# A group's choice of experts in two parts around a tile's decay, and the ranking of the experts behind the second expert's first block

## The chip, the cores and the metric

The kernel runs on one core of one Trainium2 chip. Its time is the device time of one launch in microseconds (us), the median of the runs of one kernel. Engines are named as in the profile: PE is TensorE (PEld its weight loads), DVE is VectorE, ACT is ScalarE, POOL is GpSimd, SP is SyncE, which here only issues transfers.

## The reference

Retention with a decay per head, and a two-level mixture of experts that takes one expert for each token:

```python
scores = scale * q @ k.T                          # batch 8, heads 8, seq 576, head_dim 64
ret = scores * where(rel >= 0, gamma[h] ** rel, 0)
x = (ret @ v), heads side by side                 # 4608 tokens x 512
g_logits = x @ w_group                            # 4 groups
g_idx, g_w = argmax and its softmax share
e_logits = x @ w_expert[g_idx]                    # 4 experts in a group
e_idx, e_w = argmax and its softmax share
h = relu(x @ w1[g_idx, e_idx])                    # 512 -> 1024
out = g_w * e_w * (h @ w2[g_idx, e_idx])          # 1024 -> 512
```

## The kernel before, in words

All engines run in a written order: the helper `Ordered` (L112) pins each instruction of VectorE, ScalarE, POOL and SP behind the one issued before it in the program, and TensorE's order is the program's too. So an engine that waits holds up all that is queued behind it.

**The tile loop** (L871, `t` from 0 to 36) goes over 36 tiles of 128 tokens. In iteration `t`, TensorE sums tile t-1's products of scores and values into `px` (`av`, L816), sums the running state of tile t (`state`, L801), adds the earlier tokens' part to `px` (`inter`, L834) and computes the scores of tile t+1 (`scores`, L760 and L772). VectorE multiplies `px` with the decay into `xT` (`turned`, the one instruction that is called the decay below; the next tile's `av` writes the same PSUM) and masks the scores of tile t+1 out of PSUM into `sT` (`masked`; the scores of tile t+2 write the same PSUM). ScalarE scales the values (`vs`), copies the state (`st`) and copies turned rows with their weight (`xt`). Tile t-6 is turned back (`xnat`, L369) and its rows are stored to a list per expert in HBM (`xs`) by POOL.

Three tiles are a group. Two iterations after its last tile come its logits (`logits`, L411), one later their turning (`gate_pe`, L424), one later, in iterations 6, 9, ..., 33, and 35 for the group before the last, the choice (`choose`, L427): seven steps on VectorE, `lg`, `mx`, `df`, then `oh`, `m2`, `oh`, `ob`, and an exponential of `df` on ScalarE between them. In the same iteration the weights of the rows follow (`weigh`, five steps that end in `wt`), and TensorE's sums for the places of the rows in their lists (`places_pe`, L498 to L502), which read `ob`; the next iteration computes the places (`places`, three steps). VectorE's order in such an iteration is: choice, decay, weights, masks. TensorE's is: `av`, `state`, `inter`, scores, `xnat`, logits where due, place sums.

**The transition** (L1106 to L1164) does the last group's logits and choice and the last six tiles' stores, picks the second expert (`pick(1)`; the first one was picked earlier, and its pass 0 runs here in blocks of 128 hidden columns), pads and reads expert 1's rows. `rank_experts` (L954) is a generator in three parts on VectorE: the order of all experts, their sizes and masks, and the addresses of the padding. Its first part runs in pass 0 behind `ids(0)`, the second ahead of expert 1's block 0, the third behind block 1. `expert_of(2)` lets SP read expert 2's number from that order.

**The passes** (L1168): an expert has 8 blocks (`p`, `f`); each is `layer1` (L602, 12 products into `ph`), ScalarE's relu `hh` and VectorE's remainder `hl`, and, one block later, `layer2` (L1028 to L1030). The weights come in pieces of two blocks and are split by ScalarE (`wh`) and VectorE (`wl`) three half pieces ahead. Expert 2's padding (`xpad(2)`, POOL) is issued in block 2 of expert 1, the read of its rows (`xload(2)`, SP) in block 3, their turning (`xturn`, VectorE, which writes `xTf`) in block 5 and their split (`xsplit`, `xTh` and `xTl`) in block 6.

Of the kernel before, what the change touches and what calls it, by code (L numbers as in the profile page):

```python
# [16 lines left out]
RG = 3  # L17
# [21 lines left out]
NT = N // P  # L39
# [30 lines left out]
def moe_retention(ctx, tc, qk, kv, wgt, w1, w2, c_f, out):  # L70
# [286 lines left out]
    def xnat(t, pool_=None):  # L357
        xnat_pe(t, pool_)
        xnat_out(t)
        xnat_store(t)  # L360
# [60 lines left out]
    def gate_pe(t):  # L421
        pl = ps_sm.tile([P, RG, P], F32, name=f"pl_{t}", tag="sm")
        for x_ in range(RG):
            pe.transpose(pl[:, x_, :], tiles[t]["lt"][:, x_, :], ident)  # L424
        tiles[t]["pl"] = pl

    def choose(t):  # L427

        pl = tiles[t]["pl"]

        def t_(nm, shape, dt=F32):
            return sm.tile([P, RG] + shape, dt, name=f"{nm}_{t}", tag=nm)

        K = G + 1
        n = RG
        lg = t_("lg", [GE])
        dve.tensor_reduce(
            lg, pl.rearrange("p r (a g) -> p r g a", a=NKC)[:, :, 0:GE], AX.X, ALU.add
        )
        lv = lg.rearrange("p r (k e) -> p r k e", e=4)  # L440
        mx = t_("mx", [K])
        dve.tensor_reduce(mx, lv, AX.X, ALU.max)
        df = t_("df", [K, 4])
        dve.tensor_tensor(df, lv, mx.unsqueeze(3).to_broadcast([P, n, K, 4]), ALU.subtract)
        ex = t_("ex", [K, 4])
        act.activation(ex, df, AF.Exp)
        oh = t_("oh", [K, 4])
        dve.scalar_tensor_tensor(
            oh.rearrange("p r k e -> p (r k) e"), df.rearrange("p r k e -> p (r k) e"), 0.0,
            rank.unsqueeze(1).to_broadcast([P, n * K, 4]), ALU.is_ge, ALU.mult,  # L450
        )
        m2 = t_("m2", [K])
        dve.tensor_reduce(m2, oh, AX.X, ALU.max)
        dve.tensor_tensor(
            oh, oh, m2.unsqueeze(3).to_broadcast([P, n, K, 4]), ALU.is_equal
        )
        tiles[t]["rt"] = ex, oh
        ob = obs[-1][:, 1:, :]
        dve.tensor_tensor(
            ob.rearrange("p r (g e) -> p r g e", g=G), oh[:, :, 1:, :],  # L460
            oh[:, :, 0, :].unsqueeze(3).to_broadcast([P, n, G, EG]), ALU.mult,
        )
# [42 lines left out]
    def places(t):  # L505
        n = RG
        ob = obs[-1]
        of = ob[:, 1:, :]
        pp = tiles[t]["pp"]
        pr = sm.tile([P, n, E], F32, name=f"pr_{t}", tag="pr")  # L510
        dve.tensor_tensor(pr, pp, of, ALU.mult)
        sl = sm.tile([P, n], I32, name=f"sl_{t}", tag="sl")
        with nc.allow_low_precision("integers below 2 ** 24"):
            dve.tensor_reduce(sl, pr, AX.X, ALU.add)
        tiles[t]["sl"] = sl
        more_counts()
        with nc.allow_low_precision("integers up to 36"):
            dve.tensor_reduce(counted(), ob.rearrange("p r e -> p e r"), AX.X, ALU.add)
# [121 lines left out]
    with ExitStack() as ac:  # L640
# [218 lines left out]
        def due(t, lag):  # L859

            u = t - lag
            return last_of_group(u) and u != NT - RG - 1 or u + 1 == NT - RG - 1

        def group_end(t, lag):
            return t - lag + (t - lag + 1 == NT - RG - 1)
# [5 lines left out]
        for t in range(NT + 1):  # L871
            if t + LOADS - 1 < NT:
                loads(t + LOADS - 1, "a")
            now = t < NT
            r = t - PICK

            if due(t, 4):
                choose(group_end(t, 4))
            if now and due(t, 5):
                places(group_end(t, 5))  # L880
            if r == 8:
                without()
            if t + 1 < NT:
                scale(t + 1)
            if t:
                av(t - 1)
            if t + LOADS - 1 < NT:
                loads(t + LOADS - 1, "b")
            if now:
                state(t)  # L890
            if t == NT:
                places_pe(NT - RG - 1)
                places(NT - RG - 1)
            if t:
                inter(t - 1)
                turned(t - 1)
            if r == 6:
                taken()
                close()
            if due(t, 4):  # L900
                weigh(group_end(t, 4))
            if t + 1 < NT:
                scores(t + 1)
                masked(t + 1)
            late_consts(t)
            if now and 6 <= t:
                xnat_pe(t - 6)
                xnat_out(t - 6)
            if now and due(t, 2):
                logits(group_end(t, 2))  # L910
            if due(t, 3):
                gate_pe(group_end(t, 3))
            if now and last_of_group(t - 4):
                places_pe(t - 4)

            u = t - 6
            while 0 <= u and "sl" in tiles[tiles[u]["grp"][-1]] and not tiles[u].get("out"):
                tiles[u]["out"] = True
                u -= 1
            for u in range(max(u + 1, 0), t - 5):  # L920
                if now:
                    xnat_store(u)
            if r == 5:
                pick(0)
                expert_of(0)


            if r == 6:
                xload(0)
            if 7 <= r <= 10:  # L930
                load_piece(r - 7)
            if r == 9:
                xturn(0, 0, 2)
                xturn(0, 1, 2)
# [167 lines left out]
    ranks = rank_experts()  # L1102
    L = NT - 1


    for t in range(NT - RG, NT):  # L1106
        xnat_rows(t)
    xnat(L - 5)
    xnat(L - 4, ps_sm)
    pick(1)  # L1110
    expert_of(1)
    load_piece(4)
    load_piece(5, (0,))
    logits(L)
    layer1(0, 0, 0)
    gate_pe(L)
    layer1(0, 0, 1)
    choose(L)
    xnat(L - 3)
    layer1(0, 1, 0)  # L1120
    weigh(L)
    places_pe(L)
# [20 lines left out]
    split(5)  # L1143
    layer2(0, 2)
    ids(0)
    next(ranks)
    layer1(0, 4)
    split(6)
    layer2(0, 3)
    layer1(0, 5)  # L1150
    split(7)
    expert_of(2)
    layer2(0, 4)
    width_of(1)
    for i in range(3):
# [12 lines left out]
    for p in range(1, E):  # L1168
        for f in range(NFC):
            pc = p * NPIECE + f // 2  # L1170
            if (p, f) == (1, 0):
                next(ranks)
            for i in range(pc + 3, pc + 5) if f % 2 == 0 else ():
                if i not in raws and (i >= len(pieces) or pieces[i][0] in ereg):
                    load_piece(i)
            layer1(p, f)
            turn_first = f == 0 and p > 1
            if (p, f) == (1, 0):
                split(10)
            if not turn_first:  # L1180
                split(2 * pc + f % 2 + 3)
            layer2(*prev)
            if turn_first:
                for i in range(NKC):
                    yturn(p - 1, i)
                split(2 * pc + f % 2 + 3)
            elif f == 0:
                for i in range(2):
                    finish(0, i)
            if (p, f) == (1, 1):  # L1190
                next(ranks, None)
            if f == NFC - 3 and p < E - 1:
                width_of(p + 1)
            if (p, f) == (1, 3):
                ids(1)
            if p > 1 and f > 0:
                for b in range(2 * (f - 1), 2 * f):
                    if b < nblocks(p - 1):

                        pool.tensor_copy(pace, hts[p, f][0][0:1, 0:1].bitcast(F32))  # L1200
                    ystore(p - 1, b)
            if (p, f) == (1, 2):
                xpad(2)
                sp.dma_start(cf[:, KC_TRI:KC], c_f[:, KC_TRI:KC])
            if (p, f) == (1, 3):
                xload(2)
            if f == 4 and p and p + 2 <= E:
                xpad(p + 2)
            if f == 5 and p:
                xload(p + 2)  # L1210
            if (p, f) == (2, 3):
                ov = overflow_places(cp)
                ovt = overflow_tables(*ov, mp, phs, cnt, cf, req, ident, ones, pe, dve)
            if p in (2, 3):
                next(ovt, None) if (p, f) >= (2, 3) else None
            if f == NFC - 3 and p:
                for i in range(3):
                    xturn(p + 1, i, 3)
            if f == NFC - 2 and p:
                for kc in range(NKC):  # L1220
                    xsplit(p + 1, kc)
            if f == NFC - 1 and 0 < p < E - 1:
                ids(p + 1)
            if (p, f) in ((5, NFC - 1), (10, NFC - 1), (14, NFC - 1), (E - 1, NFC - 2)):

                pool.drain(fusable=False)
            prev = (p, f)
# [297 lines left out]
```

## Time and profile before

| | us |
|---|---|
| median of 3 timed runs (573.87 to 577.48) | 574.49 |
| profiled execution, its own time | 570.59 |
| its span, from the first to the last instruction | 568.8 |
| of it the tile loop, from the scores at 8.92 to the last products | 138.44 |
| of it the transition, to expert 1's first block at 174.54 | 27.18 |
| of it expert 1's pass, to 203.01 | 28.47 |

The profile is of one execution on the chip. Times in it count from the first instruction. A row of the timeline is one instruction or a run of like ones; an idle time of the engine ahead of it, and what the profile takes to have ended it, stand in brackets. Ends of matmuls are modelled.

### The profile page before, as it was taken

To read this page: it belongs to the slowest core of one execution; us is meant where nothing else is said; L and a number is where in the kernel's file an instruction comes from. 1 tells how busy PE (TensorE), PEld (TensorE's weight loads), DVE (VectorE), ACT (ScalarE), POOL (GpSimd) and SP (SyncE) were. 2 spreads that over 40 slices of the span, in tenths; PEclk is the share of its full clock that TensorE was granted. 3 is DMA by queue.
4 is the path that set the end of the run, shared out by engine and by line. 5 is a ranking of instruction groups with operands and counts; after the bars stand their busy time and mean duration, and the time that the engine had idled before them with its cause. 6 is when DMAs were issued, how large, how long until landed. Compare 5 with 4: busy or idle time off the path is not lost.

```text
span 568.8 us, 16896 instructions
## 1 busy us (share of the span) xinstructions
PE 552.8 (97%) x6069; PEld 521.9 (92%) x6069; DVE 426.7 (75%) x999; ACT 329.3 (58%) x857; POOL 263.0 (46%) x391
## 2 busy tenths in 40 slices
PE   8999998999999999999999999999999999999995
PEld 6888877887779999999999999999999999999994
DVE  4887766888799677967777686867868677687784
ACT  5777886878467454544545455555555455555563
POOL 0022332333521128473746547383664836648555
PEclk9999999999999999999999999999999999999999
DMA  8999999789778781929383855839376584855851
GB/s 310 416 396 332 347 361 334 288 296 316 252 218 328 182 315 50 352 68 338 86 315 86 316 175 233 273 130 343 103 305 186 215 279 155 327 170 227 278 230 46
DMA packets 62251, 141.84 MB, mean 249 GB/s; under 512 B 9410, under 2 KB 30154, under 8 KB 62145
## 3 DMA queue, kind: packets, MB, share of 16 engines
q1 hardware_dynamic: 52800, 120.12, 60.2%
q0 software_dynamic: 9200, 20.21, 9.5%
q8 instruction: 73, 1.20, 0.8%
q14 instruction: 34, 0.27, 0.1%
q10 hardware_dynamic: 144, 0.05, 0.1%
HBM read 120.15 MB, written 24.75 MB: 255 GB/s over the span
## 4 chain that ended last, share of the span: by engine, by line
PE 84%; DVE 8%; DMA 2%; issue 2%; ACT 1%; POOL 1%; SPq 0%; POOLq 0%; ACTq 0%; DVEq 0%
PE ph L602 33%; PE py L1030 11%; PE py L1028 11%; PE py L1029 11%; PE px L816 5%; PE pss L772 3%; PE pst L801 2%; PE px L834 2%; PE pxt L369 2%; DVE sT L123 2%; PE plt L411 2%; PE pss L760 1%; DVE wl L123 1%; DVE xT L123 1%; DMA b<-in_kv 1%
## 5 line engine op out<-in xcount | busy, mean ns | idle before, releaser
L123 POOL DMA_INDIRECT out<-y,ii x151 | 165.9, 1099 | 61.6 <-issue 27.1
L123 DVE TENSOR_TENSOR wl<-r,wh 128x512 fp32r<-128x512 f32 x268 | 172.2, 684 | 2.8
L123 ACT ACTIVATE hh<-ph 128x356 fp32r<-128x356 f32 (+16 forms) x128 | 53.7, 419 | 184.1 <-PE ph L602 131.1
L123 ACT CAST wh<-r 128x512 fp32r<-128x512 f32 x268 | 151.4, 618 | 0.0
L602 PE MATMUL ph<-xTh_m,wh 128*128 128x316 f32 (+12 forms) x504 | 147.3, 292 | 0.0
L602 PE MATMUL ph<-xTl_m,wh 128*128 128x316 f32 (+12 forms) x504 | 147.0, 292 | 0.1
L602 PE MATMUL ph<-xTh_m,wl 128*128 128x316 f32 (+12 forms) x504 | 147.0, 292 | 0.0
L1030 PE MATMUL py<-hl,wh 128*128 128x316 f32 (+10 forms) x480 | 140.4, 293 | 0.0
L1028 PE MATMUL py<-hh,wh 128*128 128x316 f32 (+11 forms) x480 | 140.2, 292 | 0.0
L1029 PE MATMUL py<-hh,wl 128*128 128x316 f32 (+10 forms) x480 | 140.1, 292 | 0.0
L123 DVE SCALAR_TENSOR_TENSOR hl<-ph,hh 128x356 fp32r<-128x356 f32 (+15 forms) x126 | 58.2, 462 | 87.4 <-ACT hh L123 86.9
L602 PEld LDWEIGHTS ph<-xTl_m,wh 128*128 128x128 f32 x504 | 94.9, 188 | 1.0 <-DVE xTl_m L123 0.5
L602 PEld LDWEIGHTS ph<-xTh_m,wh 128*128 128x128 f32 x504 | 95.0, 188 | 0.7 <-issue 0.3
L602 PEld LDWEIGHTS ph<-xTh_m,wl 128*128 128x128 f32 x504 | 95.0, 188 | 0.0
L1030 PEld LDWEIGHTS py<-hl,wh 128*128 128x128 f32 x480 | 90.4, 188 | 0.0
L1028 PEld LDWEIGHTS py<-hh,wh 128*128 128x128 f32 x480 | 90.4, 188 | 0.0
L1029 PEld LDWEIGHTS py<-hh,wl 128*128 128x128 f32 x480 | 90.4, 188 | 0.0
L123 POOL COPY pace<-hh 1x1 f32<-1x1 f32 x140 | 35.0, 250 | 118.9 <-ACT hh L123 110.6
L123 POOL DMA_INDIRECT xs<-xt,sl x33 | 32.8, 994 | 99.5 <-DVE xT L123 38.1
L123 ACT ACTIVATE vs<-b,cf 128x64 f32<-128x64 f32 x288 | 72.4, 336 | 7.5 <-DMA b<-in_kv 6.1
L123 DVE TENSOR_TENSOR sT<-pss,masks 128x512 f32<-128x512 f32 x72 | 46.0, 681 | 13.2 <-PE pss L760 6.6
L816 PE MATMUL px<-sT,vs 128*64 128x128 f32 x576 | 40.3, 283 | 1.2 <-DVE xT L123 1.0
(194 smaller groups left out, 603.0 us busy)
## 6 DMA issues: line engine op xcount, KB each, us to landing
r<-in_w SPq DMA_DIRECT2D x138, 512.0 KB, 6.6
a<-in_qk SPq DMA_DIRECT2D x35, 512.0 KB, 7.3
b<-in_kv SPq DMA_DIRECT2D x31, 512.0 KB
xb<-xs SPq DMA_DIRECT2D x20, 165.0 KB, 3.8
xb<-xs SPq DMA_DIRECT2D x20, 148.5 KB, 3.6
out<-y,ii POOLq DMA_INDIRECT x151, 3.4
xb<-xs SPq DMA_DIRECT2D x12, 181.5 KB, 7.9
b<-in_kv SPq DMA_DIRECT2D x6, 256.0 KB
```

What stands on the lines that cost most here:

```text
L123: i_ = f(*a, **k)
L369: pe.transpose(T["pxt"][:, i, :], T["xT"][:, i, :], ident)
L411: pe.matmul(plt[32 * i : 32 * i + 32], wgp[:, i, :], tiles[t]["xTg"][:, i], start=True, stop=True)
L602: pe.matmul(ph[:, :wn], a[:, kc, cs], b[:, kc, x0 : x0 + wn], start=n == 0, stop=n == 3 * NKC - 1)
L760: pe.matmul(pss[:, o, i * P : i * P + P], T["kT"][r, i, :], T["qT"][r, i, :], start=True, stop=True,)
L772: pe.matmul(pss[k_, o, (i + par) * P + late * D : (i + par) * P + to], T["kT"][r, i + par, k_], T["qT"][r, i + par, late * D : to], start= ...
L801: pe.matmul(pst[o * D : o * D + D, i, :], T["k"][:, h, :], T["vs"][:, h, :], start=first and i == 0, stop=True, skip_group_check=True,)
L816: pe.matmul(px[g * D : g * D + D, o, s * P : s * P + P], T["vs"][:, 4 * s + 2 * g + o, :], T["sT"][:, o, 2 * s + g, :], start=s == 0, stop ...
L834: pe.matmul(px[g * D : g * D + D, o, s * P + r * w : s * P + r * w + w], st[rows, 2 * s + g, :], T["qT"][rows, 2 * s + g, r * w : r * w + ...
L1028: pe.matmul(py[:, :w0], wh[:, f % 2, ds_], hh[:, :w0], start=st_, stop=False)
L1029: pe.matmul(py[:, :w], wl[:, f % 2, ds_], hh[:, :w], start=False, stop=False)
L1030: pe.matmul(py[:, :w], wh[:, f % 2, ds_], hl[:, :w], start=False, stop=sp_)
```

## The change

The function `choose` becomes a generator that stops after the exponential. In the tile loop its first part runs where the choice was, its second part behind the decay. In the last iteration the places of the group before the last are computed behind the decay. In the transition the two `xnat` with their stores come ahead of the iotas of the last three tiles, the logits come ahead of the pick, and tile 32's `xnat` ahead of the second half of the first block and the choice. The ranking leaves pass 0 and the start of expert 1's block 0: its three parts run behind blocks 0, 1 and 2 of expert 1, and expert 2's number is read behind the first of them.

```diff
@@ choose
         act.activation(ex, df, AF.Exp)
+        yield
         oh = t_("oh", [K, 4])
@@ tile loop
-            if due(t, 4):
-                choose(group_end(t, 4))
+            choice = choose(group_end(t, 4)) if due(t, 4) else iter(())
+            next(choice, None)
             if now and due(t, 5):
                 places(group_end(t, 5))
...
                 places_pe(NT - RG - 1)
-                places(NT - RG - 1)
             if t:
                 inter(t - 1)
-                turned(t - 1)
+                if t == NT:
+                    turned(t - 1)
+                    places(NT - RG - 1)
+                else:
+                    turned(t - 1)
+                    next(choice, None)
@@ transition
+    xnat(L - 5)
+    xnat(L - 4, ps_sm)
     for t in range(NT - RG, NT):
         xnat_rows(t)
-    xnat(L - 5)
-    xnat(L - 4, ps_sm)
+    logits(L)
     pick(1)
     expert_of(1)
     load_piece(4)
     load_piece(5, (0,))
-    logits(L)
     layer1(0, 0, 0)
     gate_pe(L)
+    xnat(L - 3)
     layer1(0, 0, 1)
-    choose(L)
-    xnat(L - 3)
+    for _ in choose(L):
+        pass
     layer1(0, 1, 0)
...
     ids(0)
-    next(ranks)
     layer1(0, 4)
...
     split(7)
-    expert_of(2)
     layer2(0, 4)
@@ passes
-            if (p, f) == (1, 0):
-                next(ranks)
             for i in range(pc + 3, pc + 5) if f % 2 == 0 else ():
...
-            if (p, f) == (1, 1):
+            if p == 1 and f < 3:
                 next(ranks, None)
+                if f == 0:
+                    expert_of(2)
```

## Rows read from the trace of the kernel before

**Rows 1.** Windows: length, busy us (instructions) of each engine, granted clock, DMA share, GB/s
```profile
8.92:147.36 138.44, 131.79 (x2889) 111.57 (x2890) 105.36 (x299) 103.31 (x364) 36.33 (x64) 1.00 0.93 344
147.36:174.54 27.18, 26.61 (x176) 20.87 (x170) 22.94 (x72) 17.17 (x39) 8.08 (x13) 1.00 0.76 248
174.54:203.01 28.47, 28.47 (x187) 28.13 (x188) 23.32 (x53) 16.40 (x34) 4.54 (x4) 1.00 0.81 239
```

**Rows 2.** Timeline of iteration t = 18: start, us, engine, line, operation [idle before]
```profile
75.04 0.22 DVE L123 TENSOR_TENSOR df<-lg,mx 128x60 f32<-128x60 f32 x1
...
75.30 0.26 DVE L123 SCALAR_TENSOR_TENSOR oh<-df,cf 128x60 f32<-128x60 f32 x1
...
75.41 0.69 PE L834 MATMUL px<-a,st 64*64 64x64 f32 x32
...
76.10 0.21 DVE L123 TENSOR_TENSOR ob<-oh 128x48 bf16<-128x48 f32 x1
...
76.22 0.68 DVE L123 TENSOR_TENSOR xT<-px,gq 128x512 f32<-128x512 f32 x1
...
76.83 0.20 DVE L123 TENSOR_REDUCE sw<-ex 128x15 f32<-128x60 f32 x1
...
77.19 0.19 PE L498 MATMUL pp<-ob,up 128*128 128x48 bf16 x1
...
77.76 1.26 DVE L123 TENSOR_TENSOR sT<-pss,masks 128x512 f32<-128x512 f32 x2
...
78.82 0.69 PE L801 MATMUL pst<-vs,b 128*64 128x64 f32 x16 [0.32 <-ACT xt L123]
...
79.44 0.34 PE L772 MATMUL pss<-a 64*64 64x128 f32 x4
```

**Rows 3.** DMA queues, 76.5 to 76.7; timeline of TensorE in t = 21 and 23
```profile
q8 instruction: 1, 0.02, 29.6%
...
91.52 0.68 PE L801 MATMUL pst<-vs,b 128*64 128x64 f32 x15 [0.46 <-issue]
...
98.38 0.55 PE L772 MATMUL pss<-a 64*64 64x128 f32 x13 [1.36 <-issue]
```

**Rows 4.** Timeline: decay and next scores of t = 9 and t = 27
```profile
41.80 0.68 DVE L123 TENSOR_TENSOR xT<-px,gq 128x512 f32<-128x512 f32 x1
...
44.79 0.90 PE L772 MATMUL pss<-a 64*64 64x128 f32 x32
...
112.76 0.68 DVE L123 TENSOR_TENSOR xT<-px,gq 128x512 f32<-128x512 f32 x1
...
115.61 0.90 PE L772 MATMUL pss<-a 64*64 64x128 f32 x32
```

**Rows 5.** Timeline: the logits in t = 33, the last tile's products
```profile
137.75 0.85 PE L411 MATMUL plt<-xT,wgp 128*32 128x384 f32 x8 [0.65 <-DVE xT L123]
...
145.48 0.33 PE L816 MATMUL px<-sT,vs 128*64 128x128 f32 x2 [0.98 <-DVE xT L123]
```

**Rows 6.** Timeline: expert 1's padding, its first product
```profile
158.91 1.20 POOL L123 DMA_INDIRECT xs<-zero,pad  x1 [0.30 <-DVE wl L123]
...
174.54 0.19 PEld L602 LDWEIGHTS ph<-xTl_m,wh 128*128 128x128 f32 x1 [0.50 <-DVE xTl_m L123]
```

**Rows 7.** Timeline of VectorE and SP: ranking, expert 2's rows; the page's DMA issues
```profile
166.79 0.42 DVE L123 TENSOR_REDUCE order<-kk 128x16 int32<-128x256 f32 x1
...
187.71 0.53 DVE L123 SCALAR_TENSOR_TENSOR hl<-ph,hh 128x356 fp32r<-128x356 f32 x1 [1.41 <-ACT hh L123]
...
187.11 1.84 SPq L123 DMA_DIRECT2D xb<-xs  x2
...
196.47 1.16 DVE L123 STREAM_TRANSPOSE xTf<-xb 128x384 f32<-128x384 f32 x2
...
xb<-xs SPq DMA_DIRECT2D x20, 165.0 KB, 3.8
...
xb<-xs SPq DMA_DIRECT2D x12, 181.5 KB, 7.9
```

## The prediction

> **What bounds the kernel now.** I read the stretches first, then the timeline of single tiles. In the three stretches that the change touches TensorE is busy nearly all the time, at the full granted clock of 1.00 [rows 1], so a change is worth only what it removes or adds as waits of TensorE. From expert 1's first block (174.54 us) on TensorE is gapless; the gaps are in the tile loop and the transition, and the change works there. What matters in the loop is one iteration of three, the one that holds the choice of a group (t = 6, 9, 12, ..., 33 and 35: eleven). Its VectorE queue in t = 18 runs: three steps of the choice, four more, the decay, the weights, the masks [rows 2]. The reader should see three things there. The decay (xT) starts at 76.22, while the sums that it reads (L834) end at 75.41 + 0.69 = 76.10: the choice ends just when TensorE is done, and costs the decay almost nothing. The place sums (L498) start at 77.19, 0.88 after `ob`, which they read, was written (76.10 + 0.21). And the next scores (L772) start at 79.44, 0.42 after the masks that free their PSUM end (77.76 + 1.26 = 79.02). So `ob` has 0.88 to spare, the masks 0.42, the decay nothing that is wanted.
>
> **Part one, the choice cut in two.** Nothing is added; four VectorE steps move behind the decay. From the start of the first (75.30) to the start of the decay (76.22) they take 0.92, and `ob` is written 1.01 after the first starts; the decay holds the queue for 76.83 - 76.22 = 0.61 [rows 2]. The three steps left in front end at 75.04 + 0.22 = 75.26. VectorE then stands idle until the sums end at 76.10, because it takes its queue in order: 0.84 that the four steps filled before. The decay starts at 76.16, 0.06 earlier, and `ob` is ready at 76.16 + 0.61 + 1.01 = 77.78. The place sums, with the next tile's products and everything else of TensorE queued behind them, start at 77.84 instead of 77.19: **a new wait of 0.65**. What hid `ob` before was the transposes and the scores ahead of the place sums; that cover is 0.88 long and the move is 1.5. The weights and the masks move by 0.92 - 0.06, so the masks end at 79.88 and the scores can start at 79.93 instead of 79.44.
>
> What passes on is the later of the two, for t = 18 less what is given back: 0.32 of idle time follows before the state sums at 78.82 [rows 2]. The row names ACT's xt as what ended it, but these sums do not read it; a packet of the instruction queue falls at 76.6 [rows 3], 2.2 ahead, and such idle stretches stand 2.2 to 2.4 behind such packets in t = 9, 15 and 21 too. I take the hole for a late block of instructions, which a wait of 0.65 swallows; then TensorE is 0.33 late and the masks decide, +0.49. In t = 21 the hole is 0.46 [rows 3], and +0.2 is left. The Trainium skill, "Runtime: NRT & Kernel Launch", section "Instruction fetch mechanics", has engines fetch instructions in 16 KiB blocks ahead of use, the crossing mostly hidden. The packet has that size, but the trace shows idle time behind it; were it hidden, nothing would be swallowed, and as an estimate the sum would be 0.8 higher.
>
> The other tiles by the same steps. In t = 9 the decay started at 41.80 and cannot start earlier; the masks then end 2.80 + 0.92 behind it and the scores can start at 45.57, not 44.79: +0.8. In t = 27: 112.70 + 3.77 = 116.47 for 115.61, +0.9 [rows 4]. In t = 12 and 24 the masks have room and the place sums decide, +0.65 each; t = 15 has a hole of 0.2 and gets +0.45. In t = 30 and t = 6 the choice had made the decay wait, so it starts earlier and the masks lose less: +0.3 and +0.1, worked in the same view. Nine tiles: 0.1 + 0.8 + 0.65 + 0.45 + 0.5 + 0.2 + 0.65 + 0.9 + 0.3 = **+4.5**. TensorE is the bound after each of them, so I let all of it pass on.
>
> Two tiles gain. In t = 33 the logits wait 0.65 for the decay [rows 5], which no longer stands behind the four steps of 0.92; but a block of instructions is due about then, so I take -0.4, with bounds 0 and -0.8. In t = 35 the products of the last tile wait 0.98 for the decay [rows 5], which the four steps held up; 0.8 of it goes.
>
> **Part two, the transition.** The decay of the last tile moves ahead of the places; the logits move ahead of the pick, the stores of two tiles ahead of four iotas on POOL, and the turning of tile 32 ahead of the choice. No instruction is new. What ends this stretch is a chain: the last stores go out on POOL back to back, then expert 1's padding (158.91), its rows are read back on SP's queue, turned, and expert 1's first product waits 0.50 for them at 174.54 [rows 6]. TensorE's own savings are worth only what this chain moves. Its head is the last choice, which follows the last decay and the logits. The 0.8 of t = 35 arrives there, reduced by the pick, which now shares VectorE with the choice, and by a first iota on POOL that waits for an earlier store. With t = 35 in it I take **-0.8**, bounds -0.3 and -1.3.
>
> **Part three, the ranking.** Its three parts (about 2.9, 1.6 and 1.4; the long steps take 0.42 each) leave pass 0, where they stood in front of nothing that ends the chain of rows 6, and stand behind blocks 0, 1 and 2 of expert 1. A block lasts 3.5 and VectorE then idles 1.41 of it [rows 7]. So 5.9 of work meets some 4.2 of idle time; the remainders (hl) of blocks 1 and 2 come just when TensorE wants them: +0.1. The issues behind it: reading expert 2's number on SP now waits for the ranking, and behind it on that queue stand the weights of pieces 8 and 9, one constant and expert 2's rows. Expert 2's padding on POOL waits for the third part, which is one block (3.5) and the backlog (1.6) later, 5.1 in all, and the first read of the rows, at 187.11 before [rows 7], comes at 192.2. The turning of these rows started at 196.47 without a wait [rows 7], so they had landed within 9.4 of the first read. By that bound they land by 201.6 now. The median of this size, 7.9 to landing from one issue [rows 7], gives some 200; reads a little smaller land in 3.8, half of that: some 198.5. VectorE, in order, waits for them, with a remainder and a split queued behind. Expert 2's first product, at 203.0 [rows 1], has about 2.4 of slack for it: the turning (1.8), a remainder (0.53), a split (1.29) and the first low part (0.5) need 4.1 of the 6.5. So a wait of 2.0 costs nothing, 3.6 costs 1.2, 5.1 costs 2.7. Before, nothing else was left on the queue when the rows were read, so I take a wait near the lower end, +0.3; with the remainders **+0.4**, bounds 0 and 2.8. The weights of pieces 8 and 9 are read some 14 later, but are first split behind block 5, more than three blocks (10.5) after; that costs nothing, and without this lead would cost a microsecond for each that they are late.
>
> **Sum:** 4.5 - 0.4 - 0.8 + 0.4 = +3.7 on the profiled execution, whose own time is 570.59 and span 568.8. The median of the timed runs is 574.49; the difference carries over to it: 578.2, say 578.0.
>
> **Rivals.** *Swallowed waits, not slower:* TensorE also idles in other tiles, in the middle of the scores, 1.36 in one of four such places, for no reason that the profile shows [rows 3]. If these are holes of instruction delivery that goes by the clock and not by TensorE's progress, the new waits are paid out of them. Then the +4.5 is gone and -0.8 remains: 573.7. For it: the holes of rows 3 look alike. Against it: a block that is called for when TensorE reaches a place in its program is late by as much as TensorE is. It decides where the holes after a choice are as long as the wait. *Expert 2's rows late, slower by over 1%:* the reads land as late as the bound allows, VectorE waits 5.1 at the turning, and TensorE pays 2.7 at 203: 574.49 + 4.5 - 0.4 - 0.8 + 2.8 = 580.6, and 581.0 if t = 33 gives nothing. It decides from a landing 2.4 after the turning's turn. For it: the 7.9 median; against it: the shorter reads. *The transition carries more:* if the last choice's chain moves by TensorE's whole saving (0.98 and 0.65 in rows 5, the 0.50 of rows 6 and about 0.7 more) and the waits are swallowed too, 570.5 to 572.
>
> **How the numbers follow.** The forecast, slower by 0.2 to 0.95% (575.5 to 580), 0.56; swallowed waits (572.5 to 575.5) 0.20; late rows (580 to 583) 0.19; the larger gain 0.05, half of it beyond 1%. The range leaves out the last of these, the lowest part of the second and the upper part of the third: 573.0 to 581.5. One per cent (5.7) is about what a measurement of this kernel can tell from no change; most of the forecast lies inside it. Faster by over 1% has 0.03, slower 0.21 (the late rows and the upper tail of the forecast), within it 0.76.
>
> **What would show it.** In t = 9 to 27: VectorE idle some 0.8 between df and xT, and L498 idle some 0.6 on `ob`. In t = 33 and 35 L411 and the last L816 without their waits. The span from the first product to expert 1's first longer by about 3.3. An idle VectorE of about 2 in front of expert 2's turning, and TensorE gapless or nearly so at its first product. The prediction is wrong if L498 starts in these tiles where it did, if the scores of the next iteration catch up, or if TensorE stands at 203.

## The result and the profile after

The changed kernel takes 581.18 us (median of 8 runs, 578.13 to 585.5); the kernel before took 575.14 on the same chip (8 runs, 572.64 to 577.48). The ratio is 1.0106, with a 95% interval of 1.0068 to 1.0144: 6.0 slower. The forecast was 578.0, that is 3.5 to 3.7 slower, with a range of 573.0 to 581.5. The direction and the range held; the size came out near the upper end, in the band (580 to 583) that the prediction gave to its rival of late rows with a chance of 0.19, and the main reason is one term of the sum.

The profiled execution after is the slowest of the eight (585.5, span 583.7) and that of the kernel before, with 570.59, lies below all eight of its runs, so their stretches differ by more than the change is worth and are checked below on second profiles. Of the 14.9 between the spans, 3.2 lie behind expert 2's second block, where nothing was changed. The windows that answer to [rows 1] (length, busy time of each engine with instructions, granted clock, DMA share, GB/s), from the first scores to the last products, to expert 1's first block, to expert 2's:

```profile
9.77:154.06 144.29, 136.62 (x2890) 114.07 (x2890) 103.32 (x296) 102.83 (x364) 35.60 (x62) 0.99 0.90 326
154.06:182.15 28.09, 26.59 (x176) 20.89 (x170) 21.20 (x66) 17.06 (x39) 8.91 (x15) 1.00 0.74 234
182.15:214.08 31.93, 29.67 (x186) 29.05 (x187) 24.36 (x58) 16.38 (x34) 4.23 (x4) 0.97 0.71 190
```

The loop is 5.85 longer, the transition 0.91, expert 1's pass 3.46; and that pass, gapless before, now has 31.93 - 29.67 = 2.26 in which TensorE does nothing; most of the other 1.2 is a lower clock, as shown below.

In the loop, t = 18 answers to [rows 2] (timeline: start, length, engine, line; idle time ahead and what ended it in brackets; L499 and L773 were L498 and L772):

```profile
78.99 0.22 DVE L123 TENSOR_TENSOR df<-lg,mx 128x60 f32<-128x60 f32 x1
...
80.33 0.95 PE L773 MATMUL pss<-a 64*64 64x128 f32 x31 [0.34 <-issue]
...
80.62 0.69 DVE L123 TENSOR_TENSOR xT<-px,gq 128x512 f32<-128x512 f32 x1 [1.41 <-PE px L835]
...
81.98 0.21 DVE L123 TENSOR_TENSOR ob<-oh 128x48 bf16<-128x48 f32 x1
...
82.25 0.18 PE L499 MATMUL pp<-ob,up 128*128 128x48 bf16 x1 [0.38 <-DVE ob L123]
...
83.05 1.26 DVE L123 TENSOR_TENSOR sT<-pss,masks 128x512 f32<-128x512 f32 x2
...
84.36 0.90 PE L773 MATMUL pss<-a 64*64 64x128 f32 x32 [0.34 <-DVE sT L123]
```

Both waits of the prediction stand there: L499 on `ob`, and the next scores on the masks. VectorE idles 1.41 ahead of the decay, not 0.8; the half microsecond more goes with an idle stretch in the middle of the scores (0.34 <-issue): the decay starts only behind it, 0.68 after its sums end (79.72 + 0.22).

At the end of the loop, the logits of t = 33, the last tile's products and the last decay, which answer to [rows 5]:

```profile
145.19 0.85 PE L411 MATMUL plt<-xT,wgp 128*32 128x384 f32 x8
...
152.18 1.09 PE L817 MATMUL px<-sT,vs 128*64 128x128 f32 x16 [0.23 <-issue]
...
155.09 0.69 DVE L123 TENSOR_TENSOR xT<-px,gq 128x512 f32<-128x512 f32 x1 [1.09 <-PE pxt L369]
```

The logits' 0.65 is gone and the products wait 0.23 for 0.98, as said.

Expert 2's rows, which answer to [rows 7]: weights, padding and reads on SP's and POOL's queues, the turning on VectorE, and TensorE's first product that needs a remainder behind it:

```profile
191.60 2.07 SPq L123 DMA_DIRECT2D r<-in_w  x4
...
196.68 0.98 POOL L123 DMA_INDIRECT xs<-zero,pads  x1 [6.79 <-DVE el L123]
...
197.96 1.27 POOL L123 DMA_INDIRECT xs<-zero,pads  x1 [0.30 <-issue]
...
201.10 1.89 SPq L123 DMA_DIRECT2D xb<-xs  x4
...
209.12 1.76 DVE L123 STREAM_TRANSPOSE xTf<-xb 128x384 f32<-128x384 f32 x3 [5.02 <-DMA xb<-xs]
...
211.35 0.42 PE L1035 MATMUL py<-hl,wh 128*128 128x332 f32 x1 [2.26 <-DVE hl L123]
```

VectorE stands 5.02 at the turning, and TensorE pays 2.26 for it. That is the rival "expert 2's rows late" (5.1 and 2.7). TensorE stands in expert 1's last block, though, whose products with `hl` need the remainder queued behind the turning, and not at expert 2's first product as the prediction had it. The granted clock then falls; windows of after:

```profile
208.33:211.92 3.59, 1.33 (x10) 1.07 (x9) 2.80 (x6) 1.01 (x3) 0.00 (x0) 1.00 1.14 228
211.92:215.33 3.41, 3.41 (x14) 3.41 (x14) 3.41 (x8) 2.00 (x5) 0.00 (x0) 0.50 1.16 232
```

At 0.50 (1.2 GHz for 2.4) the rest of expert 1's last block, up to 213.82, and then the start of expert 2's first block run. That first block takes 4.25 instead of 3.57; what the low clock costs in both is worked out at c_rank below.

### The profile page after: what moved, and what is told of

Same layout as the page of the kernel before. It is cut to its first block, busy times and chain, and to the rows that moved or that the text cites. A ratio compares the mean times of both kernels' runs of the same rounds, so it can differ in the third digit from the quotient of the medians.

```text
span 583.7 us, 16898 instructions
## 1 busy us (share of the span) xinstructions
PE 559.6 (96%) x6069; PEld 525.1 (90%) x6069; DVE 425.5 (73%) x999; ACT 328.5 (56%) x857; POOL 261.4 (45%) x391
## 4 chain that ended last, share of the span: by engine, by line
PE 80%; DVE 9%; DMA 5%; issue 3%; POOL 1%; SPq 1%; ACT 0%; another core or an unknown queue 0%; POOLq 0%; DVEq 0%
PE ph L603 29%; PE py L1035 10%; PE py L1033 10%; PE py L1034 10%; PE px L817 6%; PE px L835 3%; PE pss L773 3%; PE pxt L369 2%; PE pst L802 2%; DMA xb<-xs 2%; PE plt L411 2%; DVE wl L123 2%; PE pss L761 1%; DMA a<-in_qk 1%; DVE xT L123 1%
## 5 line engine op out<-in xcount | busy, mean ns | idle before, releaser
L123 DVE TENSOR_TENSOR xT<-px,gq 128x512 f32<-128x512 f32 x36 | 24.7, 687 | 29.6 <-PE px L835 24.0
```

The source lines that it names most:

```text
L123: i_ = f(*a, **k)
```

## The experiments

Three sets ran on three chips (medians of the kernel before: 579.58, 569.09, 574.73); each ratio is to before on its own chip. Lengths are worked from timeline starts: of the decays of tiles 1, 31 and 35, and of the second blocks of experts 1 and 2.

| kernel (set) | tile 1 to 31 | 31 to 35 | 35 to (1, 1) | (1, 1) to (2, 1) | ratio, 95% interval |
|---|---|---|---|---|---|
| before, first profile | 114.59 | 15.91 | 30.32 | 28.60 | |
| after, first profile | 121.41 | 16.07 | 30.35 | 32.63 | 1.0106 [1.0068, 1.0144] |
| a_split (1) | 121.65 | 16.27 | 30.29 | 28.60 | 1.0079 [1.0035, 1.0123] |
| b_trans (1) | 116.79 | 17.06 | 30.16 | 28.52 | 1.0022 [0.9977, 1.0066] |
| c_rank (1) | 116.19 | 17.14 | 29.72 | 31.47 | 1.0039 [0.9992, 1.0086] |
| d_split_pp (1) | 122.44 | 16.30 | 30.30 | 28.52 | 1.0061 [1.0020, 1.0101] |
| before_again (2) | 112.49 | 15.88 | 29.93 | 28.52 | |
| e_ab (2) | 116.25 | 14.55 | 31.32 | 28.52 | 1.0024 [1.0005, 1.0044] |
| f_rank12 (2) | 114.83 | 14.54 | 30.52 | 30.13 | 1.0081 [1.0053, 1.0109] |
| h_behind (2) | 115.51 | 15.59 | 29.58 | 28.52 | 1.0030 [1.0014, 1.0046] |
| g_late (3) | 116.38 | 16.08 | 30.13 | 28.52 | 1.0004 [0.9974, 1.0035] |
| k_ob (3) | 114.86 | 16.72 | 30.44 | 28.60 | 1.0009 [0.9980, 1.0038] |
| l_whole (3) | 130.26 | 17.82 | 30.14 | 28.52 | 1.0275 [1.0238, 1.0311] |
| after_again (3) | 121.03 | 16.02 | 30.22 | 33.30 | 1.0174 [1.0135, 1.0212] |

**One part each.** a_split, b_trans and c_rank put one of the three parts into the kernel before, with hunks of the diff ahead:

```diff
 a_split: choose and the tile loop, without the places behind the last decay
+        yield
...
+                next(choice, None)
 b_trans: the transition, and in iteration 36
+                    places(NT - RG - 1)
 c_rank: the passes
-            if (p, f) == (1, 0):
-                next(ranks)
...
+            if p == 1 and f < 3:
                 next(ranks, None)
+                if f == 0:
+                    expert_of(2)
```

> The kernel before with the choice cut in two and nothing else. Theory of the prediction (place sums wait for ob, and the next scores for the later masks): 3 to 5 us slower than before; L498 idle 0.5 to 0.75 on ob in t = 9 to 30, VectorE idle about 1.4 ahead of the decay there, the logits of t = 33 and the products of t = 35 without their waits. Rival (the longer loop in the changed kernel's one profile is a late start and instruction delivery, and the whole 6 us are the ranking's): within 1 us of before, with waits at L498 that are given back later in the same group.

> The kernel before with the transition's new order alone (places of the group before the last behind the last decay, logits ahead of the pick, stores ahead of the iotas, tile 32 turned ahead of the choice). Theory of the prediction, with the gain of t = 35 left out: within 0.5 us of before, since the last choice's chain shares VectorE with the pick and ends no earlier. Rival (the transition's chain moves by TensorE's savings): 1 to 2 us faster.

> The kernel before with the ranking alone moved behind blocks 0, 1 and 2 of expert 1. Theory that expert 2's rows land late: VectorE idle 3 to 5 us ahead of their turning, TensorE idle about 2 to 3 us in expert 1's block 6 or 7, then a stretch at half the granted clock; 2.5 to 4.5 us slower. Theory that the prediction held (reads land early): at most 1 us slower, no idle of TensorE above 0.5. Rival that the loop explains everything: within 0.5 us of before.

The two kernels with an uncut choice take 116.79 and 116.19 from tile 1 to 31, the cut one 121.65: 5.2 more, for a forecast of 4.5. From tile 31 to 35 it gives back 0.8. The transition moves nothing: in b_trans the stretch to (1, 1) is 30.16, for 29.72 and 30.29 where its order is the old one. The ranking alone costs 2.95 in expert 1's pass. So the loop and the rows are the two losses, and the transition is none. The turning and TensorE in c_rank, with the loop as before:

```profile
202.35 1.76 DVE L123 STREAM_TRANSPOSE xTf<-xb 128x384 f32<-128x384 f32 x3 [5.42 <-DMA xb<-xs]
...
204.58 0.42 PE L1030 MATMUL py<-hl,wh 128*128 128x332 f32 x1 [2.66 <-DVE hl L123]
```

Its clock stays at 1.00, so it gives the price of the low clock in after. Without the wait, expert 1's last block takes 6.45 - 2.66 = 3.79 here and 6.95 - 2.26 = 4.69 in after; expert 2's first block takes 3.58 and 4.25. Together the clock costs about 1.6.

**Place sums one tile later.** d_split_pp is a_split with the place sums and the places behind the next tile's products, so that no place sum waits for `ob`:

```diff
+            if now and due(t, 5):
+                places_pe(group_end(t, 5))
+                places(group_end(t, 5))
...
-            if now and last_of_group(t - 4):
-                places_pe(t - 4)
```

> As a_split, with the place sums moved behind the next tile's products, so that ob has the time that it needs; the computation is the same. If the place sums' wait is the cost: 1 to 3 us faster than a_split, what is left being the masks' 0.5 to 0.9 in t = 9, 18 and 27. If the masks (0.9 later in each of the nine tiles) are the cost: within 1 us of a_split.

The loop does not recover: 122.44 for 121.65, and the timed runs differ by no more than their intervals (1.0061 for 1.0079). What its profiled execution of 587.76 has over a_split's of 584.34 lies behind expert 2's second block. Its t = 18:

```profile
81.48 0.20 PE L499 MATMUL pp<-ob,up 128*128 128x48 bf16 x1
...
83.02 0.90 PE L773 MATMUL pss<-a 64*64 64x128 f32 x32 [0.62 <-DVE sT L123]
```

L499 no longer waits, and the scores wait 0.62 for the masks instead of 0.34. Two waits lie one behind the other, and the later one decides.

**Both out of the way.** h_behind puts the second part and the weights behind the masks, and the place sums behind the next tile's state sums:

```diff
             if t + 1 < NT:
                 scores(t + 1)
                 masked(t + 1)
+            next(choice, None)
+            if due(t, 4):
+                weigh(group_end(t, 4))
```

> The kernel before with the choice cut in two, its second part and the weights behind the masks of the next tile, and the place sums with the places one tile later, behind that tile's state sums. So neither the place sums nor the masks are later than in the kernel before. Theory (two waits, the masks' and the place sums', either of which alone keeps the loss): the loop from tile 1's decay to tile 34's is 129.5 to 131.5, as in the two kernels with the loop unchanged (131.10 and 130.58), against 134.21 and 135.06 with the choice cut in two; ratio 0.998 to 1.003. Rival (something else in the cut: the decay that idles 1.4 us ahead of it, or the turned rows that now wait for their weights on ScalarE): the loop stays at 133 to 135, ratio 1.006 or more.

On its chip the expected lengths don't apply as they stand (the kernel before takes 112.49 to tile 31 there, not some 116.5), so it is held against the cut kernels of its own set: 115.51, between their 114.83 and 116.25. It does not recover, so the theory that the two waits are all of it falls. In its t = 18 and 19:

```profile
77.75 1.28 DVE L123 TENSOR_TENSOR sT<-pss,masks 128x512 f32<-128x512 f32 x2
...
79.70 0.21 DVE L123 TENSOR_TENSOR ob<-oh 128x48 bf16<-128x48 f32 x1
...
79.96 0.18 PE L499 MATMUL pp<-ob,up 128*128 128x48 bf16 x1 [0.34 <-DVE ob L123]
...
80.67 0.17 DVE L123 RECIPROCAL wt<-we 128x3 f32<-128x3 f32 x1
80.76 0.66 DVE L123 TENSOR_TENSOR xT<-px,gq 128x512 f32<-128x512 f32 x1
81.03 0.69 ACT L123 ACTIVATE xt<-pxt,wt 128x512 f32<-128x512 f32 x1 [2.54 <-DVE wt L123]
...
81.78 0.66 PE L369 MATMUL pxt<-cf,xT 128*128 128x128 f32 x4 [0.70 <-ACT xt L123]
```

The masks are early, but VectorE now works without a gap up to the next tile's decay, which starts 1.60 behind its sums for 0.95 in the kernel before, and even the later place sums wait for `ob`. A wait stands here that no other kernel has: the weights `wt` end only at 80.84, ScalarE's `xt` waits 2.54 for them, and TensorE's next turning (L369), which writes the PSUM that `xt` reads, waits 0.70 for it. Between the decays of tiles 1 and 31 this takes 3.9 in eight iterations, and the waits on `ob` take 1.9. That is the second half of the rival, the turned rows that wait for their weights. So h_behind has put other waits in the place of the masks' wait; whether an order without any of them would recover the loss is not shown.

**How much is moved.** In set 3 the cut stands in four places: nowhere up to t = 30 (g_late, cut only in 33 and 35), ahead of the last step (k_ob), where the change has it (after_again), ahead of the first step (l_whole):

```diff
 g_late
+            if t < 33:
+                for _ in choice:
+                    pass
+            next(choice, None)
 k_ob, in choose
         tiles[t]["rt"] = ex, oh
+        yield
         ob = obs[-1][:, 1:, :]
 l_whole, behind turned(t - 1)
+                for _ in choice:
+                    pass
```

> The kernel before with the choice cut in two only in iterations 33 and 35, where all seven steps had held the decay up. Theory (the cut costs where the choice ended just with TensorE's sums and gains where it ended behind them): up to tile 31's decay nothing changes; from tile 31's decay to tile 34's 11.5 to 12.6 instead of 13.1 to 14.4; the rest as before; 1.0 to 1.5 us less, ratio 0.997 to 0.999. Rival (what TensorE gains there the transition's chain of stores gives back, as in the changed kernel, where the stretch to expert 1's second block came out 0.3 to 0.8 shorter): ratio 0.999 to 1.001.

> The kernel before with the choice cut one step ahead of its end, in every group: six steps ahead of the decay, only the one that writes ob behind it. Theory (ob had 0.88 to spare ahead of the place sums in the profile of before): ob moves by the decay's 0.61 and a little, which the spare time covers, and the masks by nothing, so no place sums wait; the loop up to tile 31's decay stays within 1 us of the kernel before, some 3 to 5 below the changed kernel's on the same chip; 31 to 34 gains 0.2 to 0.3; ratio 0.998 to 1.001. Rival (any step behind the decay is paid for, since VectorE has no time to spare there): +0.25 in each of nine tiles, some 2 us, ratio 1.003 to 1.004.

> The kernel before with the whole choice behind the decay, in every group: all seven steps, 1.75 us, instead of four, 0.92. Theory (the later of place sums and masks decides, and each step moved is paid in full): the place sums wait 0.65 + 0.83 = 1.5 in each of the nine tiles, the loop up to tile 31's decay is some 12 us longer than before, 7 longer than the changed kernel's on the same chip; ratio 1.015 to 1.022. Rival (the waits are mostly paid out of idle stretches that TensorE has anyway, and a few us is all that such a tile can lose): the loop within 3 us of the changed kernel's, ratio 1.004 to 1.010.

> The changed kernel once more, unchanged, beside the three others on one chip. Theory (late rows of expert 2 and place sums that wait): VectorE idles 4.5 to 5.5 in front of expert 2's turning, TensorE 2.3 to 2.9 at expert 2's first low part, the stretch from expert 1's second block to expert 2's second is 31.4 to 32.7; the loop to tile 31's decay is 3 to 5 longer than in the late cut; from tile 31's decay to tile 34's 11.6 to 12.5; ratio 1.009 to 1.013. Whether the clock falls behind that idle time, as in the first profile and not in the kernel with the ranking alone, is open: if it is the length of the idle time (2.42 and 2.82) it does not decide. Rival (the first profile's wait at expert 2 was one execution's): the stretch is below 29.5, ratio about 1.004.

Windows of the four, from tile 1's decay to tile 31's: g_late, k_ob, after_again, l_whole.

```profile
16.26:132.64 116.38, 112.66 (x2457) 94.62 (x2459) 88.21 (x251) 87.47 (x311) 30.33 (x53) 1.00 0.92 337
```
```profile
17.07:131.93 114.86, 112.17 (x2457) 94.97 (x2459) 86.97 (x252) 86.43 (x307) 30.57 (x53) 1.00 0.93 337
```
```profile
16.91:137.94 121.03, 113.72 (x2457) 95.02 (x2459) 86.78 (x251) 86.49 (x306) 30.53 (x53) 1.00 0.89 319
```
```profile
18.25:148.51 130.26, 114.98 (x2457) 96.20 (x2459) 87.78 (x251) 86.47 (x305) 30.30 (x53) 0.99 0.83 296
```

The work is the same (2457 matmuls) and the length beyond it grows: 3.7, 2.7, 7.3, 15.3. One step behind the decay costs nothing; four cost 121.03 - 116.38 = 4.65; seven cost 13.88, two more than the theory's 12. The t = 18 of k_ob and l_whole show why:

```profile
78.33 0.20 DVE L123 TENSOR_TENSOR ob<-oh 128x48 bf16<-128x48 f32 x1
...
78.80 0.19 PE L499 MATMUL pp<-ob,up 128*128 128x48 bf16 x1
```
```profile
87.17 0.21 DVE L123 TENSOR_TENSOR ob<-oh 128x48 bf16<-128x48 f32 x1
...
87.42 0.20 PE L499 MATMUL pp<-ob,up 128*128 128x48 bf16 x1 [1.33 <-DVE ob L123]
```

In k_ob `ob` still comes 0.27 before it is wanted (78.80 - 78.53). In l_whole the sums wait 1.33. So the spare time that the prediction read from [rows 2] is there, and what is moved beyond it is paid in nearly every group. The late cut alone is no gain that can be measured (1.0004): from tile 31 to 35 it is 16.08, for 16.72 in k_ob and 17.06 to 17.14 in set 1, so 0.6 to 1 us (the kernel before has no profile in this set), but the timed runs do not resolve it.

after_again repeats the wait behind expert 2's rows: VectorE 5.62, TensorE 2.86, and the clock after it:

```profile
208.54 1.76 DVE L123 STREAM_TRANSPOSE xTf<-xb 128x384 f32<-128x384 f32 x3 [5.62 <-DMA xb<-xs]
...
210.78 0.42 PE L1035 MATMUL py<-hl,wh 128*128 128x332 f32 x1 [2.86 <-DVE hl L123]
```
```profile
211.31:214.72 3.41, 3.41 (x15) 3.41 (x14) 3.41 (x9) 2.04 (x5) 0.00 (x0) 0.50 1.12 254
```

Its ratio, 1.0174, lies above the 1.009 to 1.013 expected, and above the upper end of the prediction's range (581.5 to 574.49 is 1.012); why this chip pays more than the first pair, with 1.0106, is open. Against g_late on the same chip the spans differ by 9.9: 4.65 to tile 31, 4.78 in the pass, 0.65 ahead of tile 1, and the rest cancels.

**Expert 2's rows.** e_ab is the whole change with the ranking where it was; f_rank12 is the whole change with the third part, which gives the padding's addresses, one block earlier:

```diff
-            if p == 1 and f < 3:
+            if p == 1 and f < 2:
                 next(ranks, None)
                 if f == 0:
                     expert_of(2)
+                else:
+                    next(ranks, None)
```

> The whole change except the ranking, which stands where it was (first part in pass 0, second ahead of expert 1's block 0, third behind block 1). Theory (late rows of expert 2): the stretch from expert 1's second block to expert 2's second, 32.63 in the changed kernel, is 28.5 to 28.7 again, TensorE has no idle time at expert 2's first product, and the ratio to the kernel before is about 1.004 to 1.006, that is 3 us below the changed kernel. Rival (all of the loss is in the tile loop, and the wait at expert 2's first product only takes the place of one that comes later anyway): the stretch is shorter, but the time stays within 1 us of the changed kernel, ratio 1.010.

> The whole change, but the ranking's third part, which gives the padding addresses, stands behind the second, in block 1 of expert 1, one block (3.5 us) earlier. Theory (what costs is the chain padding, landing, read of 8.0 us, turning): the padding goes out at about 193 instead of 196.7, the first read at about 197.5, the turning of expert 2's rows idles about 1.5 instead of 5.0, TensorE does not idle at expert 2's first product, its clock stays at 1.00, and the stretch from expert 1's second block to expert 2's second is 28.6 to 29.4 instead of 32.63; ratio 1.004 to 1.007. Rival (the 5.9 us of ranking on VectorE delay the remainders and splits of the pass themselves): the stretch stays above 31. Second rival (the read queues behind the weights, so its end does not move with its start): the turning still idles over 4.

> The kernel before once more, unchanged, for a second profile. Theory (the 127.75 of the first profile's loop from tile 1's decay to tile 34's is one of the low ones; short idle stretches of TensorE in the scores fall differently from one execution to the next): the loop is 129.5 to 131.5 and the span 572 to 576, with more tiles whose decay starts 0.7 behind its sums. Rival (the loop of this code is 127.75 within 0.5, and the 131.10 and 130.58 of the kernels with an unchanged loop come from the edits behind it): the loop is 127.3 to 128.3, the span about 569.

e_ab has 28.52 again and no wait, as the theory had it, and its ratio of 1.0024 is below the 1.004 expected, on the chip where the cut costs least. The second profile of before was shorter than either theory had it on this chip (112.49 to tile 31, 125.62 to tile 34, span 566.1), so it is the measure for set 2 and says nothing on set 1. f_rank12 agrees with none of the three theories in full. In f_rank12 the padding went out 1.65 earlier relative to (1, 1) (9.59 for 11.24), and the first read did not come earlier (15.87, for 15.66 in after, 16.68 in after_again and 16.29 in c_rank):

```profile
186.06 1.25 POOL L123 DMA_INDIRECT xs<-zero,pads  x1 [0.31 <-issue]
...
191.06 1.89 SPq L123 DMA_DIRECT2D xb<-xs  x4
...
197.89 1.76 DVE L123 STREAM_TRANSPOSE xTf<-xb 128x384 f32<-128x384 f32 x3 [2.91 <-DMA xb<-xs]
```

SP waits for the padding's landing there. What the queues carry meanwhile (packets, MB, share of the 16 DMA engines; q1 is SP's queue, q0 POOL's), in f_rank12 from 184.8 to 188.6, the 3.8 us behind the first padding, and in the first profile of before from 184.6 to 187.2, the 2.6 us behind it:

```profile
q1 hardware_dynamic: 329, 1.08, 95.2%
q0 software_dynamic: 3, 0.01, 0.8%
```
```profile
DMA packets 80, 0.07 MB, mean 29 GB/s; under 512 B 62, under 2 KB 62, under 8 KB 80
...
q0 software_dynamic: 80, 0.07, 8.6%
```

Before, the padding's 80 packets had the engines to themselves. Now expert 2's number is read only behind the ranking, so the four weight loads of pieces 8 and 9, 512 KB each, are issued at 191.60 in after, 5 us ahead of the padding, and fill the engines when it is issued; three of its packets move in 3.8 us. In after it is the same: from 196.6 to 198.6, with SP's queue at 99.1%, one of POOL's packets moves, and 153 in the 2.0 us behind, as SP's queue runs down. The Trainium skill, "DMA: Bandwidth & Descriptors", section "Queues, rings and completion order", says that an engine takes turns between the queues that have work, a packet from each; by that the padding would have moved beside the weights. The rows do not show it; whether its descriptors were late or its packets were held is open. No kernel was run with the weights elsewhere, so that they are the cause is argued from these rows and from the read that did not move with the padding.

With 2.91 at the turning TensorE does not idle behind it, as expected. But the stretch is 30.13: VectorE's two parts in block 1 cost TensorE 0.57 at a remainder, and from there its matmuls ran at a longer pitch (below). Its ratio, 1.0081, is above the expected 1.004 to 1.007.

## Why the prediction was right, and where not

- **Part one, up to t = 30: +4.5.** Right in place, and in size within what the chips differ by: 4.65 against g_late, 5.2 against b_trans and c_rank; 3.0 in set 2 (mean of e_ab and f_rank12 less before_again); the two first profiles differ by 6.8. That the masks' wait alone keeps the loss is shown by d_split_pp, that the spare time decides by k_ob and l_whole. The steps follow two readers of what is moved, the place sums and the masks; h_behind shows a third, the turned rows through their weights, which decides once the weights move far enough.
- **t = 33 and 35: -0.4 and the 0.8.** From tile 31 to 35 the cut gives back 0.8 in set 1 (16.27 against 17.06 and 17.14) and 1.3 in set 2 (14.55 against 15.88), for 1.2 in the sum, and nothing between the two first profiles (16.07 against 15.91). How much of it a block of instructions ate in t = 33 can't be told from these.
- **Transition: -0.8.** The new order adds nothing to the gain of t = 35: from its decay to (1, 1) it takes 30.16 to 31.32 (five kernels), the old one 29.58 to 30.44 (nine). Where the new order follows a cut choice on set 2's chip, part of the 1.3 is lost again. So little of the 1.2 reaches expert 1: from tile 31's decay to (1, 1) the new code takes 46.42 for 46.23 in the two first profiles, and 45.87 and 45.06 for 45.81 in set 2.
- **Ranking: +0.4.** This is the step that failed: "so I take a wait near the lower end, +0.3". Measured: 2.95 with the ranking alone, 4.0 and 4.8 in the two profiles of the whole change, 1.6 of each the clock, for which the prediction has no term. Two readings went wrong. The rows took 8.0 from first read to turning (209.12 - 201.10), the 7.9 of [rows 7] and not half of it; that the queue was empty before was no reason for the shorter one. And the first read came 6.4 later relative to (1, 1) (15.66 for 9.29), not 5.1: from the padding's issue to the read it took 4.4 (201.10 - 196.68) for 2.5 before (187.11 - 184.61). The weights of pieces 8 and 9, which I had costed at nothing because VectorE needs them late, are the likely cause, as argued above. The price of a late landing was nearly right: a slack of about 2.4 was read, and 5.02 - 2.26, 5.42 - 2.66 and 5.62 - 2.86 each leave 2.76, but at the remainder of expert 1's block 6 and not at expert 2's first product.
- **Rivals.** *Expert 2's rows late* is what happened. *Swallowed waits* falls: the chips whose profiles show idle stretches in the scores behind the choice (sets 1 and 3) pay 4.65 to 5.2 for the cut, the one without pays 3.0. *The transition carries more* falls with it.

The forecast with the rival's 2.8 in place of 0.4 is 580.6, near the 581.18 measured, but that is partly luck: the clock's 1.6 is not in it, the 1.2 that it takes off hardly came, and set 3's chip shows a larger loss. That the range held is luck in the same measure.

## What to carry to other kernels

Before work is moved behind a step, read how long every reader of its results can wait, those further down the queue too, and move no more than that. A transfer that is moved can count twice, at its own deadline and at the deadline of a transfer beside which it now runs. Where a row gives the time of a transfer under the load that it will meet, take that row, not the shorter one.

## What the runs showed of the hardware

- Behind TensorE's idle 2.26 and 2.86 in the two profiles of the changed kernel the granted clock fell to 0.50 for 3.41; behind 2.66 in c_rank it stayed at 1.00. The length of the idle time alone does not decide it.
- In f_rank12, from the late remainder in (1, 3) on, matmuls without any wait and at a granted clock of 1.00 took longer from start to start for twelve blocks. Windows over the same six blocks of expert 2, f_rank12 and before_again:

```profile
208.91:230.51 21.60, 21.60 (x147) 21.60 (x145) 15.89 (x41) 10.48 (x22) 16.14 (x24) 1.00 0.52 172
```
```profile
207.23:227.87 20.64, 20.64 (x146) 20.64 (x145) 15.43 (x40) 10.46 (x23) 16.40 (x24) 1.00 0.29 77
```

  That is 3.60 for 3.44 a block, some 2 us in all. A short stretch of the like stands in every kernel behind expert 1's first product (in before block 2 of expert 1 takes 3.67 and block 4 takes 3.52, both without a wait), but only f_rank12 has it for twelve blocks. Its cause is open.
- The same loop code differs by chip and execution: 112.49 and 114.59 from tile 1 to 31 in the two profiles of the kernel before, 116.2 to 116.8 in sets 1 and 3. In the longer ones TensorE idles some 0.35 within the scores behind the choice, and the decay starts 0.66 to 0.76 behind its sums instead of 0.07 to 0.15. The execution that the prediction was read from was of the shorter kind, and the forecast's difference held all the same.
